# Two attention problems on one core: the gate exponential behind the first scores, first loads in order of need, all partial output sums ahead of the last two key blocks, the flag behind the last evacuations

## The chip, the cores and the metric

The kernel runs on one core of one Trainium2 chip. Times are device microseconds (us) of one execution. A median is over several executions of the same kernel. A profile is the trace of one such execution; its span is about 2 us shorter than the time measured from outside (906.0 for 907.87 us in the profiled run of after).

Engines: PE = TensorE matmul, PEld = TensorE weight load, DVE = VectorE, ACT = ScalarE, POOL = GpSimd, SP = SyncE (a name with q, such as SPq, is that engine's sequencer, which also issues DMAs). In these traces each engine runs its instructions in the order of the program, and an instruction that waits holds up everything behind it (in before, the kA cast, whose input is ready near 9 us, starts at 13.13, behind the gate exp that waits for beta until 13.02).

## The reference, cut to what matters

Two attention layers over 2048 tokens, width 512, 32 heads of 16. Problem A works in 4 segments of 512 with a causal softmax in each, and adds a read from a memory that earlier segments filled. Problem B is plain attention over all 2048 tokens. The outputs stand side by side.

```python
phi = lambda t: jnp.where(t > 0, t + 1.0, jnp.exp(t))
g = sigmoid(beta)                                # one gate per head
for s in range(4):                               # problem A
    p = softmax(qs @ ks.T * scale + mask)
    a_dot = p @ vs
    pq = phi(qs)
    a_mem = (pq @ M) / (pq @ z + 1e-06)          # memory of earlier segments
    outs.append(g * a_mem + (1.0 - g) * a_dot)
    pk = phi(ks)
    M = M + pk.T @ vs                            # first needed in segment 1
    z = z + pk.sum()
...                                              # then @ wo
b = softmax(q @ k.T * scale) @ v                 # problem B, then @ wo
```

## The kernel before

The exponentials of the scores are most of the work of ScalarE. Scores lie in PSUM in two tiles, one of 1536 columns and one of 1024 (the exps of the traces read 128x1536 and 128x1024; the program counts 3 and 2 banks, so a bank in this text is 512 columns), so that PE fills one while ScalarE empties the other. Some score blocks are exponentiated by VectorE with integer arithmetic instead (tiles `v_ps` and `vx`). The program builder keeps a model of time (`T["pe"]`, `T["act"]`, `T["dve"]`, `T["pool"]`) and, while it emits instructions, picks for each gap in PE's work the "chore" (a projection, an evacuation, a memory update) that fits. The result is a fixed order for each engine; nothing is decided on the chip.

The first loads and the start. `ld(queue, which, lo, hi)` loads columns of wq (0), wk (1) or wv (2):

```python
START = 8.4
ARRIVE = dict(wv=13.0, wk=15.3, wq=16.5, xb=(20.5, 26.0, 31.5, 37.0), wvb=24.0)   # model: when loads are there
...
ld(nc.scalar, 1, 0, P)
ld(nc.scalar, 0, 0, P)
xTA = {0: load_xT(wk, "a", 0, "xTA", 1)}         # 4 DMA transposes on SyncE's queue
nc.scalar.activation(warm[:], ones_b[:], ACT.Exp)
load_beta()                                      # 4 small loads, ScalarE's queue
ld(nc.sync, 2)
ld(nc.sync, 1, P)
ld(nc.sync, 0, P)
...                                              # B's weights, 16 DMA transposes of B's x, wo_a, wo_b: all SyncE
for cc in range(4):
    for i in range(2):
        mm(ps0[i][:], wA[1 - i][:, cc, 0:P], xTA[0][:, cc, :], start=(cc == 0), stop=(cc == 3))
pin(nc.scalar.activation(gcol[:], beta_t[:], ACT.Exp, scale=-1.0))     # gate: waits for beta
pin(nc.scalar.copy(kA[0, 0][:], ps0[0][:]))                            # kA: the first scores wait for it
for e in range(2):
    pin(nc.vector.tensor_scalar(qA[0, 0][:, e, :], ps0[1][:], par[:, e:e + 1], None, ALU.mult))
```

The memory's phi(k), which is not part of the change but matters below. `ex` is ScalarE's exp, `po` and `pk` (the tile named phkT) are VectorE's, and four DMA transposes on SyncE's queue turn phkT into `phk` for PE. There is one buffer of phkT; two row tiles of the same segment follow each other through it:

```python
def phase1(wk, src, dst, then):                  # cut: queueing
    ex = wk.tile([P, W], F32, name="ex", tag="ex")
    pin(nc.scalar.activation(ex[:], src, ACT.Exp))
    ...
    pin(nc.vector.tensor_scalar(po[:], src, 0.0, None, ALU.max))
    pin(nc.vector.scalar_tensor_tensor(dst, ex[:], 1.0, po[:], ALU.min, ALU.add))

def do_phik(wk, k, out, then=None):
    pk = wk.tile([P, W], BF16, name="phkT", tag="phkT")
    def move():
        ph = out["ph"] = wk.tile([P, 4, P], BF16, name="phk", tag="phk", bufs=2)
        for kb in range(4):
            nc.sync.dma_start_transpose(ph[:, kb, :], pk[:, kb * P:(kb + 1) * P])
        if then is not None:
            then()
    phase1(wk, k, pk[:], move)
    yield
...
held["pk"] = T["dve"] + 6.5                      # model: the transposes have read phkT by then
...
chore(d - 14, phik(), 1, slot=False, ok=lambda: held["pk"] < T["pe"] and held["ph"] < 2)
```

The end. The partial output sums `l_ps` take PE's time between the last key blocks, and the flag (were all softmax sums in range?) is computed ahead of the last evacuations. All engines load the flag and branch on it to a slow exact path, which these inputs never take:

```python
partial(3, ...); partial(2, ...)
while len(pvq) > 1:
    assert pv(1, True)                           # a key block of the last sums
partial(0, ...)
assert pv(1, True)                               # the last key block
partial(1, ...)
...
run(sums_ok(wk, 62, 64, okm[:, 2:3], "b"))
...
pin(nc.vector.tensor_scalar(flag[:], fps[0:1, 0:1], P - 0.5, None, ALU.is_lt))
for sb in range(4):                              # last evacuations and stores
    ...
```

## Time and profile before

| | before |
|---|---|
| median of the first three runs | 902.09 us (901.56 to 903.89) |
| profiled span | 900.1 us |
| first score exp starts | 14.41 us |
| last score exp ends | 886.94 us |
| from there to the end | 13.14 us |
| score exps on ScalarE / busy time of them | 749 / 856.8 us |

From the profile page of before, a line of the costliest groups (line, engine, operation, tiles, count | busy us, mean ns | idle us just before, and what ended most of it) and two lines of the span in 40 slices of 22.5 us (tenths of busy time; PEclk in tenths of full speed):

```profile
ACT  3899999999999999999999999999999999999994
PEclk8999999999999999999999999999999999999998
L827 ACT ACTIVATE pT<-s_ps 128x1536 bf16<-128x1536 f32 x749 | 856.8, 1287 | 8.3 <-PE s_ps L109 6.1
```

ScalarE is full in all but the first two slices and the last one. So the time is the start of the first exp, plus the exps, plus ScalarE's stalls between them, plus the tail.

The start, from the timeline of before (start us, us, engine, line, operation; in brackets the idle time before and what ended it):

```profile
9.07 1.41 DVE L1069 TENSOR_SCALAR qA<-q_ps,par 128x512 bf16<-128x512 f32 x2 [6.20 <-PE q_ps L109]
...
13.02 0.21 ACT L1066 ACTIVATE gcol<-beta_t 128x8 f32<-128x8 bf16 x1 [9.66 <-DMA beta_t<-in_A_beta_dram]
13.13 0.57 ACT L1067 CAST kA<-k_ps 128x512 bf16<-128x512 f32 x1
...
13.75 1.03 PE L109 MATMUL s_ps<-qA,kA 32*128 32x512 bf16 x6 [4.72 <-ACT kA L1067]
...
14.41 1.45 ACT L827 ACTIVATE pT<-s_ps 128x1536 bf16<-128x1536 f32 x1 [0.71 <-PE s_ps L109]
```

The cast of kA takes 0.57 us and its input was ready near 9 us, but the gate exp in front of it waits 9.66 us for beta. The first scores wait for kA.

The same wait also slows PE, which has nothing to do from 9.0 to 13.7 us: its granted clock falls to half at about 11.1 us (an estimate from one-microsecond windows: 0.56 from 11 to 12, then 0.50) and stays there until about 18 (0.53 from 17 to 18, then 1.00). The windows of PE in before (window, us, busy us and instructions, granted clock, mean DMA share, GB/s):

```profile
16.00:18.00 2.00, 2.00 (x11) 0.52 1.12 167
18.00:20.00 2.00, 2.00 (x14) 1.00 0.54 103
```

The timeline of SyncE's queue in before (the second figure is the time from the first to the end of the last of xN issues):

```profile
18.86 16.11 SPq L219 DMA_TRANSPOSE xT_b<-in_B_x_dram  x12
...
36.26 5.03 SPq L219 DMA_TRANSPOSE xT_a<-in_A_x_dram  x4
49.95 12.11 SPq L315 DMA_TRANSPOSE phk<-phkT  x5
```

And VectorE's timeline in before at the first phi(k):

```profile
48.83 0.28 DVE L289 TENSOR_SCALAR po<-kA 128x512 bf16<-128x512 bf16 x1
49.23 0.69 DVE L290 SCALAR_TENSOR_TENSOR phkT<-ex,po 128x512 bf16<-128x512 f32 x1
49.84 0.71 DVE L358 STREAM_TRANSPOSE tT<-acc 128x512 f32<-128x512 f32 x1
```

SyncE's queue has been done with its loads since 41.3 us (36.26 + 5.03) when phkT is finished at 49.92 (49.23 + 0.69), so the transposes issue at once, at 49.95. The second phkT is written at 60.2, long after they have read the buffer.

The end, from the chain of waits of before (start us, us, what):

```profile
892.69 0.03 DVE flag L1175
...
892.76 0.70 DVE osb L1179
```

The flag is done at 892.83 (its own duration is 0.14 us), and the two evacuations on VectorE come behind it.

### The profile page before, as it was taken

Reading aid. Unit: us, or ns where it says so; the run is one execution under the profiler, and the core shown is the slowest. Engines: PE = TensorE matmul, PEld = TensorE weight load, DVE = VectorE, ACT = ScalarE, POOL = GpSimd, SP = SyncE. Lnnn points to the kernel's source line nnn. Section 1 sums busy time; section 2 is a strip of 40 time slices with the busy share of each in tenths; the row PEclk is TensorE's granted clock in tenths of the full one; section 3 lists DMA queues with packets and bytes.
Section 4 is the critical chain, followed back from the end, with each engine's and each line's share of the span. In section 5 each row is a group of like instructions: output and inputs, shape, how many; then the busy total and the mean of one; then the engine's idle time right before and its main releaser. Section 6 shows DMA issues by size and latency. Waiting matters only on the chain.

```text
span 900.1 us, 18954 instructions
## 1 busy us (share of the span) xinstructions
PE 866.8 (96%) x7674; PEld 260.2 (29%) x7674; DVE 794.2 (88%) x1359; ACT 868.2 (96%) x779; POOL 152.1 (17%) x327
## 2 busy tenths in 40 slices
PE   6999999999999999999999999999999999999996
PEld 2222222232323223222232223223222222222321
DVE  1777789989898998988989999999999899999995
ACT  3899999999999999999999999999999999999994
POOL 4630120411303003030120304002030300000000
PEclk8999999999999999999999999999999999999998
DMA  7700000010000110000000010000000000000001
GB/s 185 143 13 7 24 4 5 7 25 7 7 1 14 36 30 8 1 1 7 1 7 2 25 30 1 1 1 1 2 2 1 19 30 1 2 1 2 1 2 28
DMA packets 35649, 15.47 MB, mean 17 GB/s; under 512 B 27360, under 2 KB 35552, under 8 KB 35552
## 3 DMA queue, kind: packets, MB, share of 16 engines
q1 hardware_dynamic: 33776, 13.78, 6.5%
q8 instruction: 62, 1.02, 0.5%
q10 hardware_dynamic: 1776, 0.40, 0.2%
q14 instruction: 35, 0.29, 0.1%
HBM read 4.20 MB, written 4.19 MB: 9 GB/s over the span
## 4 chain that ended last, share of the span: by engine, by line
PE 42%; ACT 31%; issue 12%; DVE 5%; POOL 2%; DVEq 0%; ACTq 0%; POOLq 0%
ACT pT L827 30%; PE acc L109 19%; PE s_ps L109 11%; PE v_ps L109 7%; POOL pT L837 2%; DVE vx L899 2%; PE o_ps L109 2%; PE k_ps L109 1%; DVE vx L915 1%; ACT ex L284 1%; PE q_ps L109 1%; PE am_ps L109 0%; DVE tT L358 0%; DVE tN L391 0%; POOL qB L259 0%
## 5 line engine op out<-in xcount | busy, mean ns | idle before, releaser
L827 ACT ACTIVATE pT<-s_ps 128x1536 bf16<-128x1536 f32 x749 | 856.8, 1287 | 8.3 <-PE s_ps L109 6.1
L899 DVE TENSOR_SCALAR vx<-v_ps 128x512 uint16<-128x512 f32 x496 | 324.7, 684 | 30.2 <-PE v_ps L109 23.8
L109 PE MATMUL s_ps<-qB,KB 32*128 32x512 bf16 x1552 | 250.7, 382 | 8.9 <-ACT pT L827 5.5
L915 DVE TENSOR_SCALAR vx<-vx 128x2048 uint16<-128x2048 uint16 x372 | 244.6, 690 | 1.9 <-PE acc L109 0.7
L109 PE MATMUL acc<-vx,VB 128*32 128x512 f16 x1984 | 181.3, 385 | 0.6 <-DVE vx L915 0.3
L109 PE MATMUL v_ps<-qB,KB 32*128 32x512 bf16 x496 | 171.4, 382 | 1.1 <-DVE vx L899 0.5
L837 POOL TENSOR_SCALAR_AFFINE_SELECT pT<-pT 128x256 bf16<-128x256 bf16 (+2 forms) x242 | 104.8, 462 | 306.0 <-ACT pT L827 304.7
L109 PE MATMUL acc<-pT,VB 128*32 128x512 bf16 x1552 | 152.8, 387 | 0.0
L109 PEld LDWEIGHTS <-KB 32*128 32x128 bf16 x2048 | 84.2, 91 | 235.8 <-issue 227.8
L109 PE MATMUL acc<-zeros 128*128 128x512 bf16 x411 | 137.1, 386 | 0.0
L109 PEld LDWEIGHTS <-VB 128*32 128x32 bf16 x3536 | 74.5, 94 | 161.7 <-issue 152.4
L109 PE MATMUL s_ps<-qA,kA 32*128 32x384 bf16 (+3 forms) x512 | 54.1, 303 | 7.7 <-ACT kA L1067 4.7
L109 PEld LDWEIGHTS <-zeros 128*128 128x128 bf16 x433 | 35.1, 98 | 84.9 <-issue 77.0
L259 POOL TENSOR_SCALAR qA<-qc,par 128x512 bf16<-128x512 bf16 x24 | 16.5, 701 | 248.6 <-DVE qc L257 248.6
L358 DVE STREAM_TRANSPOSE tT<-acc 128x512 f32<-128x512 f32 x64 | 45.0, 704 | 10.2 <-PE acc L109 9.9
L109 PE MATMUL acc<-pT,vA 128*32 128x256 bf16 (+3 forms) x512 | 32.5, 305 | 1.2 <-DVE vx L899 0.8
L109 PEld LDWEIGHTS <-kA 32*128 32x128 bf16 x512 | 17.1, 92 | 47.8 <-issue 39.7
L259 POOL TENSOR_SCALAR qB<-qc,par 128x512 bf16<-128x512 bf16 x32 | 23.6, 750 | 8.6 <-DVE qc L257 8.6
L435 DVE CAST osb<-o_ps 128x512 bf16<-128x512 f32 x28 | 19.2, 687 | 6.6 <-PE o_ps L109 6.3
L304 DVE CAST vA<-v_ps 128x512 bf16<-128x512 f32 x16 | 11.0, 689 | 11.7 <-PE v_ps L109 11.7
L257 DVE CAST qc<-q_ps 128x512 bf16<-128x512 f32 x28 | 19.2, 684 | 2.4 <-PE q_ps L109 2.1
L109 PE MATMUL k_ps<-xT_a,w_a 128*128 128x512 bf16 x64 | 19.6, 383 | 0.8 <-DMA xT_a<-in_A_x_dram 0.7
(88 smaller groups left out, 419.1 us busy)
## 6 DMA issues: line engine op xcount, KB each, us to landing
out_dram<-osb SPq DMA_DIRECT2D x31, 128.0 KB, 1.7
w_b<-in_B_wqkv_dram SPq DMA_DIRECT2D x3, 512.0 KB, 5.2
phk<-phkT SPq DMA_TRANSPOSE x48, 2.3
w_a<-in_A_wv_dram SPq DMA_DIRECT2D x1, 512.0 KB, 6.6
wo_a<-in_A_wo_dram SPq DMA_DIRECT2D x1, 512.0 KB, 4.3
wo_b<-in_B_wo_dram SPq DMA_DIRECT2D x1, 512.0 KB, 5.1
w_a<-in_A_wk_dram SPq DMA_DIRECT2D x1, 384.0 KB, 7.9
w_a<-in_A_wq_dram SPq DMA_DIRECT2D x1, 384.0 KB, 8.5
```

The lines of the kernel that those rows point to most:

```text
L109: return pin(nc.tensor.matmul(out, lhsT, rhs, **k))
L257: pin(nc.vector.tensor_copy(qc[:], ps[:]))
L259: pin(nc.gpsimd.tensor_scalar(dst[:, e, :], qc[:], par[:, e:e + 1], 0.0, ALU.mult, ALU.add))
L284: pin(nc.scalar.activation(ex[:], src, ACT.Exp))
L304: pin(nc.vector.tensor_copy(dst, ps[:].rearrange("p (h d) -> p h d", d=DH)))
L358: pin(nc.vector.transpose(st["tT"][:, e].rearrange("p c d -> p (c d)"), acc[:]))
L435: pin(nc.vector.tensor_copy(osb[:], ps[:]))
L827: pin(nc.scalar.activation(pT[:, 0:n, :], pt[:, 0:n, :], ACT.Exp, scale=SCALE))
L837: pin(nc.gpsimd.affine_select(out=blk, in_=blk, compare_op=ALU.is_ge, fill=0.0, base=0, pattern=[[0, len(sls)], [1, P]], channel_multiplie ...
L899: pin(nc.vector.tensor_scalar(x[:, j, :], vt[:], XSCALE, float(LADDER[0]), ALU.mult, ALU.add))
L915: pin(nc.vector.tensor_scalar(p[:], x[:], float(off - LADDER[0]), 32767.0, ALU.add, ALU.min))
```

## The change

The intent is to let the first scores start without beta, to bring the first weights in the order in which they are used, to keep VectorE from taking score blocks while it is behind, and to shorten the end. Below, the parts are called the gate (the gate exp behind the sixth score group), the loads (their order, with beta behind them on SyncE's queue), the debt rule (fewer score blocks for VectorE while it is behind), the aT hold (a new aT only when the one buffer is free), the GpSimd rule, the tail order (all partial sums ahead of the last two key blocks) and the flag. The diff, cut to its core:

```diff
+VLATE = 0.5
+TAILPV = 2
-ARRIVE = dict(wv=13.0, wk=15.3, wq=16.5, xb=(20.5, 26.0, 31.5, 37.0), wvb=24.0)
+ARRIVE = dict(w1=11.0, wv=13.5, wk=16.0, wq=17.0, xb=(20.5, 26.0, 31.5, 37.0), wvb=24.0)
@@ loads
-            nc.scalar.dma_start(out=beta_t[...])
+            nc.sync.dma_start(out=beta_t[...])
+        ld(nc.sync, 1, P, 2 * P)
+        ld(nc.sync, 0, P, 2 * P)
+        ld(nc.sync, 2)
+        ld(nc.sync, 1, 2 * P)
+        ld(nc.sync, 0, 2 * P)
         load_beta()
-        ld(nc.sync, 2)
-        ld(nc.sync, 1, P)
-        ld(nc.sync, 0, P)
@@ projections of A, segment 0: row tile 1 may run from w1 on
-    chore(d - LEAD, part(k()), 4, after=rel if s else ARRIVE["wk"], ...)
+    chore(d - LEAD, part(k()), 4, after=rel if s else ARRIVE["w1" if rt == 1 else "wk"], ...)
     ... (the same for q)
@@ score blocks for VectorE: fewer candidates the further it is behind
+    vmin = VMIN + VLATE * (max(0.0, T["dve"] - T["pe"]) + sum(t["us"] for t in tasks)) / QUAD
-    if u["name"] == "a" or len(u["kbs"]) < VMIN:
+    if u["name"] == "a" or len(u["kbs"]) < vmin:
@@ ... (a hold on the one aT buffer; final multiplies may go to GpSimd where the model finds it free)
@@ start
-        pin(nc.scalar.activation(gcol[:], beta_t[:], ACT.Exp, scale=-1.0))
         pin(nc.scalar.copy(kA[0, 0][:], ps0[0][:]))
@@ score loop
-                if t == 3:
-                    later(1.2, gates, prio=1)
+                if t == 6:
+                    pin(nc.scalar.activation(gcol[:], beta_t[:], ACT.Exp, scale=-1.0))
+                    later(1.2, gates, prio=1, ready=on_act(0.2, T["pe"]))
@@ end: partial sums 3 and 2, key blocks down to TAILPV, partial sums 0 and 1, the rest
-        while len(pvq) > 1:
+        while len(pvq) > TAILPV:
             assert pv(1, True)
@@ ...
-        run(sums_ok(wk, 62, 64, okm[:, 2:3], "b"))
-        ... flag
         for sb in range(4):
             ... last evacuations and stores
+        run(sums_ok(wk, 62, 64, okm[:, 2:3], "b"))
+        ... flag
```

Of the GpSimd rule only one multiply comes out in the built program.

More of the change, by code (lines that the diff above doesn't have):

```diff
@@ L58 @@
 POOLMIN = 99
+TAILPV = 2
+POOLTT = 1.2
+POOLSLACK = -99.0
+POOLWITH = 1.2
+POOLWAIT = 4.0
 LEAD = 2.5
@@ L95 @@
     ports = {k: deque(maxlen=8) for k in ("dve", "pool")}
-    held = {"tT": False, "ex": False, "qc": 0, "phi": deque()}
+    held = {"tT": False, "aT": False, "ex": False, "qc": 0, "phi": deque()}
     def mm(out, lhsT, rhs, at=0.0, **k):
@@ L181, in load_beta @@
         for j in range(4):
-            nc.scalar.dma_start(out=beta_t[32 * j:32 * j + 32, :].rearrange("p (rt e) -> p rt e", e=2),
+            nc.sync.dma_start(out=beta_t[32 * j:32 * j + 32, :].rearrange("p (rt e) -> p rt e", e=2),
                               in_=bsrc[j:j + 1].to_broadcast([32, 4, 2]))
@@ L368, in f @@
             if "aT" not in st:
+                held["aT"] = live[0]
                 st["aT"] = wk.tile([P, 2, 16, 32], F32, name="aT", tag="aT")
@@ L372, in f @@
                 then()
-        later(0.72, f, am)
+        later(0.72, f, am, ok=lambda: "aT" in st if e else not held["aT"])
     def fin_pair(wk, st, name, rt, ridx, ot):
@@ L389, in fin_pair @@
         if aT is None:
-            yield -0.75
-            pin(nc.vector.tensor_tensor(o, tT[:, :, :, 0:DH], rr.to_broadcast(bc), op=ALU.mult))
+            eng = (yield (POOLTT, 0.75)) or nc.vector
+            pin(eng.tensor_tensor(o, tT[:, :, :, 0:DH], rr.to_broadcast(bc), op=ALU.mult))
         else:
@@ L397, in fin_pair @@
             t1, t2 = tT[:, :, :, 0:DH], aT[:, :, :, 0:DH]
-            yield -0.7
-            pin(nc.vector.tensor_tensor(t1, t1, rr.to_broadcast(bc), op=ALU.mult))
-            yield -0.7
-            pin(nc.vector.tensor_tensor(t2, t2, r2[:].to_broadcast(bc), op=ALU.mult))
-            yield -0.7
-            pin(nc.vector.tensor_tensor(o, t1, t2, op=ALU.add))
+            eng = (yield (POOLTT, 0.7)) or nc.vector
+            pin(eng.tensor_tensor(t1, t1, rr.to_broadcast(bc), op=ALU.mult))
+            eng = (yield (POOLTT, 0.7)) or nc.vector
+            pin(eng.tensor_tensor(t2, t2, r2[:].to_broadcast(bc), op=ALU.mult))
+            eng = (yield (POOLTT, 0.7)) or nc.vector
+            pin(eng.tensor_tensor(o, t1, t2, op=ALU.add))
         yield 0.71
@@ L555, in project @@
                 if (s, rt) != (0, 0):
-                    chore(d - LEAD, part(k()), 4, after=rel if s else ARRIVE["wk"],
+                    chore(d - LEAD, part(k()), 4, after=rel if s else ARRIVE["w1" if rt == 1 else "wk"],
                           key=("k", "a", s, rt), ok=lambda: s == 0 or ("phk", s - 1, rt) in seen)
-                    chore(d - LEAD, part(q()), 4, after=rel if s else ARRIVE["wq"],
+                    chore(d - LEAD, part(q()), 4, after=rel if s else ARRIVE["w1" if rt == 1 else "wq"],
                           key=("q", "a", s, rt))
@@ L679, in backlog @@
             return max(0.0, T["dve"] - T["pe"]) + sum(t["us"] for t in runnable() if t["ready"] < T["pe"] + 0.6)
+        ptasks = deque()
         def in_turn(g, prio, end=None):
+            on = [None]
             def step():
-                c = next(g, None)
+                eng = on[0]
+                try:
+                    c = g.send(eng)
+                except StopIteration:
+                    c = None
+                ready = max(T["dve"], T["pool"] + 0.06) if eng else T["dve"]
+                on[0] = None
+                if isinstance(c, tuple):
+                    if T["pool"] < T["pe"] + POOLSLACK and len(ptasks) < 2:
+                        on[0] = nc.gpsimd
+                        ptasks.append((ready, c[0], step))
+                        return
+                    c = -c[1]
                 if c is not None:
-                    later(abs(c), step, prio=prio, ready=T["dve"], port=c < 0)
+                    later(abs(c), step, prio=prio, ready=ready, port=c < 0)
                 elif end is not None:
@@ L692, in pair_end @@
             held["tT"] = False
+            if u["name"] == "a":
+                held["aT"] = False
             if u["sums"] == 30:
@@ L920, in pool_run @@
         def pool_run():
+            while ptasks and max(T["pool"], ptasks[0][0]) < T["pe"] + 0.15:
+                free = sum(t["us"] for t in runnable() if not t["port"] and t["ready"] < T["pe"] + 0.3)
+                if live[0] and free < POOLWITH and T["pe"] < ptasks[0][0] + POOLWAIT:
+                    return
+                ready, us, f = ptasks.popleft()
+                on_pool(us, ready)
+                f()
             while T["pool"] < T["pe"] + 0.1:
@@ L1133 @@
                 urge()
-        while chores or cur_chore[0] or tasks or len({q["u"]["id"] for q in pvq}) > 1:
+        while chores or cur_chore[0] or tasks or ptasks or len({q["u"]["id"] for q in pvq}) > 1:
             dve_run(T["pe"])
+            pool_run()
             if cur[0] < len(units) - 1 and pv(1, True):
@@ L1154, in partial @@
                    skip_group_check=True)
-        partial(3, mp.tile([P, D], F32, name="l_ps3", tag="misc")[:])
-        partial(2, mp.tile([P, D], F32, name="l_ps2", tag="misc")[:])
-        while len(pvq) > 1:
+        last = [ps_s.tile([P, BANKS[(NT + i) % 2], 512], F32, name="l_ps", tag=f"s{(NT + i) % 2}") for i in range(1)]
+        left = [(3, lambda: mp.tile([P, D], F32, name="l_ps3", tag="misc")[:]),
+                (2, lambda: mp.tile([P, D], F32, name="l_ps2", tag="misc")[:]),
+                (0, lambda: last[0][:, 0, :]), (1, lambda: last[0][:, 1, :])]
+        for n in (1, 1):
+            sb, t = left.pop(0)
+            partial(sb, t())
+        while len(pvq) > TAILPV:
             assert pv(1, True)
-        last = ps_s.tile([P, BANKS[NT % 2], 512], F32, name="l_ps", tag=f"s{NT % 2}")
-        partial(0, last[:, 0, :])
-        assert pv(1, True)
-        partial(1, last[:, 1, :])
+        for sb, t in left:
+            partial(sb, t())
+        while pvq:
+            assert pv(1, True)
         tN = fin[("b", NSEG - 1, NRT - 1)]["tN"]
@@ L1168 @@
                skip_group_check=True)
-        run(sums_ok(wk, 62, 64, okm[:, 2:3], "b"))
-        okb = wk.tile([P, 1], BF16, name="okb")
-        pin(nc.vector.tensor_reduce(okb[:], okm[:], axis=AX.X, op=ALU.min))
-        fps = ps_a.tile([P, W], F32, name="f_ps", tag="misc")
-        mm(fps[0:1, 0:1], ones_b[:], okb[:], start=True, stop=True)
-        flag = const.tile([1, 1], I32, name="flag")
-        pin(nc.vector.tensor_scalar(flag[:], fps[0:1, 0:1], P - 0.5, None, ALU.is_lt))
         for sb in range(4):
@@ L1183 @@
             (nc.scalar if sb == 2 else nc.sync).dma_start(out=out2[r0:r0 + P, D:2 * D], in_=osb[:])
+        run(sums_ok(wk, 62, 64, okm[:, 2:3], "b"))
+        okb = wk.tile([P, 1], BF16, name="okb")
+        pin(nc.vector.tensor_reduce(okb[:], okm[:], axis=AX.X, op=ALU.min))
+        fps = ps_a.tile([P, W], F32, name="f_ps", tag="misc")
+        mm(fps[0:1, 0:1], ones_b[:], okb[:], start=True, stop=True)
+        flag = const.tile([1, 1], I32, name="flag")
+        pin(nc.vector.tensor_scalar(flag[:], fps[0:1, 0:1], P - 0.5, None, ALU.is_lt))
     def exact_problem(name):
```

## The prediction

> **What bounds the kernel now.** ScalarE's exponentials. In the groups of instructions it is busy 868.2 of 900.1 us, 856.8 of them in 749 exps. In the timeline the first exp starts at 14.41, the last ends at 886.94; between 60 and 880 us the windows show ScalarE 99 to 100% busy. So time = start of the first exp + exp work + ScalarE stalls + tail (13.2 us). Both builds have 749 exps and 124 score blocks exponentiated on VectorE (instruction counts), so the work stays; the change can only move the other three.
>
> **Start.** ScalarE's in-order stream has the gate exp, waiting for the beta loads until 13.02, ahead of the kA cast (13.13) that the first scores (13.75) need. k_ps was done at about 8.9, the first half of qA at about 9.8. With the gate exp six exps later, scores can start at 9.8 and the first exp at about 10.4: 4.0 us gained, all critical.
>
> **Front stalls.** Between 14 and 29 us ScalarE loses about 5.4 us: 1.4 before the third exp (six filler matmuls at 0.43 us, granted clock 0.5 from 11.1 to 17.9 us), 1.05 at 25.6 (mask on GpSimd), 1.74 at 28.2 (k and q of the second row tile, late). The change loads their 128-column weights first and projects them behind the first two score groups. I expect 2 to 4 us of stall left: if the PE clock still halves ([...] here 4.9 us of idle did), seven projection matmuls take 3 us ahead of the third score group; and v waits for wv, now behind 256 KB more, to about 13.3 (12.6 before). Gain 2.5. B's loads slip about 1 us; first use at about 26, landing about 24.5: tight, no stall expected.
>
> **Middle.** Block choice by VectorE's debt, the aT hold and GpSimd finish ops (only one multiply moves in the build) reorder instructions. Stalls from 30 to 850 us total roughly 15 us. Gain 0.5, give or take 2.
>
> **Tail.** Last key blocks ahead of partial sums: the same twelve l_ps matmuls (0.215 us each) and accumulations stand behind the last scores, so the last acc still ends about 2.3 us after the last exp; gain 0 to 0.5. The flag is not harmless at the end. Every engine loads it (892.9), branches (893.5 to 894.6), and resumes only at 896.7 to 898.2. [...] So the span ends by the flag, not by the last store. Behind two 0.69-us evacuations the flag comes 1.5 us later; SyncE, which branched at 894.64 behind its stores, loses only about 0.5. Cost 0.5 to 1.3.
>
> **Sum.** 902.1 - 4.0 - 2.5 - 0.5 + 0.7 = 895.8 us, range 892.5 to 898.8. Faster by over 2% (below 884) 2%, within 2% 97%, slower by over 2% 1%.
>
> **What would show it.** First exp near 10.4; no idle of 9.7 us before the gate exp; ScalarE's waits on PE before 30 us halved; last exp ending near 880; flag to end unchanged at about 7.3 us, last exp to end 13.5 to 14.5.
>
> **What would make it wrong.** Scores still starting late (qA's second half, weights landing after 11 us); B's loads stalling ScalarE after 25 us; new stalls in the reordered middle[...].

## More of the kernel before

ScalarE's timeline around the two phi(k) exps:

```profile
47.93 0.67 ACT L284 ACTIVATE ex<-kA 128x512 f32<-128x512 bf16 x1
...
58.55 0.63 ACT L284 ACTIVATE ex<-kA 128x512 f32<-128x512 bf16 x1
```

## The result, and the profile after

| | before | after |
|---|---|---|
| median | 902.34 us (901.56 to 903.89, 4 runs) | 907.74 us (905.48 to 908.84, 4 runs) |
| profiled span | 900.1 us | 906.0 us |
| first score exp starts | 14.41 | 10.82 |
| last score exp ends | 886.94 | 891.62 |
| from there to the end | 13.14 | 14.43 |

The ratio of after to before is 1.0055, with a 95% interval of 1.0031 to 1.0078: within 2%, but slower. Here and below a ratio is the mean time of one kernel's fast runs over the mean time of the other's fast runs of the same rounds, so it is not quite the ratio of the medians.

The profile page of after, the same three lines:

```profile
ACT  5969999999999999999999999999999999999994
PEclk9979999999999999999999999999999999999998
L853 ACT ACTIVATE pT<-s_ps 128x1536 bf16<-128x1536 f32 x749 | 857.6, 1281 | 15.3 <-PE s_ps L115 12.9
```

The work is the same, 749 exps and 857.6 us. What ScalarE idles ahead of exps has grown from 8.3 to 15.3 us, nearly all of it in waits for scores. The slice strings say where to look: the first slice is better (5 for 3, and a clock of 9 for 8), the third is worse (6 for 9, and a clock of 7 for 9). That is 45 to 67 us.

To see where each microsecond went I took ScalarE's instructions in order and summed, for each stretch, the time from one start to the next beyond the median period of its shape (1.331 us for the 3-bank exp, 0.904 for the 2-bank exp, 0.519 for the phi exp). This balance is worked out from the two traces:

| us | before | after | difference |
|---|---|---|---|
| first exp starts | 14.41 | 10.82 | -3.6 |
| stalls up to 45 us | 5.35 | 1.49 | -3.9 |
| gate exp, now between two score exps | 0 | about 0.5 | +0.5 |
| stalls 45 to 100 us | 2.24 | 10.06 | +7.8 |
| stalls 100 to 870 us | 15.30 | 18.46 | +3.2 |
| stalls behind 870 us | 0.07 | 0.85 | +0.8 |
| last exp to the end | 13.14 | 14.43 | +1.3 |
| sum | | | +6.1 (spans: +5.9) |

A nanosecond more or less in a median period moves the long stretch from 100 to 870 us by some tenths: redone run by run, entries of this kind move by up to 0.5 us, so smaller differences mean nothing.

The start did what it should. Timeline of after, against that of before:

```profile
9.36 0.59 ACT L1099 CAST kA<-k_ps 128x512 bf16<-128x512 f32 x1 [6.00 <-PE k_ps L115]
9.58 1.41 DVE L1101 TENSOR_SCALAR qA<-q_ps,par 128x512 bf16<-128x512 f32 x2 [6.71 <-PE q_ps L115]
10.38 0.59 PE L115 MATMUL s_ps<-qA,kA 32*128 32x512 bf16 x6 [0.84 <-DVE qA L1101]
...
10.82 2.37 ACT L853 ACTIVATE pT<-s_ps 128x1536 bf16<-128x1536 f32 x2 [0.87 <-PE s_ps L115]
```

The wait for beta is gone from the front, PE idles 0.84 us instead of 4.72, and between 8 and 20 us its granted clock stays at 1.00.

Now the third slice. ScalarE's timeline of after around the phi(k) exps:

```profile
30.68 0.67 ACT L290 ACTIVATE ex<-kA 128x512 f32<-128x512 bf16 x1
...
43.72 0.78 ACT L290 ACTIVATE ex<-kA 128x512 f32<-128x512 bf16 x1
44.24 5.70 ACT L853 ACTIVATE pT<-s_ps 128x1024 bf16<-128x1024 f32 x5
54.27 1.45 ACT L853 ACTIVATE pT<-s_ps 128x1536 bf16<-128x1536 f32 x1 [4.34 <-PE s_ps L115]
```

The first phi exp has moved from 47.93 to 30.68 us. Counted in score exps, it stands behind 16 instead of 25, and the second behind 27 instead of 34. Later comes a stall of 4.34 us. SyncE's queue in after:

```profile
19.95 17.94 SPq L225 DMA_TRANSPOSE xT_b<-in_B_x_dram  x12
...
39.18 5.04 SPq L225 DMA_TRANSPOSE xT_a<-in_A_x_dram  x4
44.31 12.94 SPq L321 DMA_TRANSPOSE phk<-phkT  x8
```

VectorE's first phkT of after starts at 33.27 us and takes 0.80. Its transposes come behind loads and issue only at 44.31, 10.2 us later; before, they issued at once. The builder's model lets the second phi(k) come 6.5 us behind the first phkT. VectorE's timeline in after then shows what follows:

```profile
44.70 0.49 DVE L295 TENSOR_SCALAR po<-kA 128x512 bf16<-128x512 bf16 x1
50.82 0.69 DVE L296 SCALAR_TENSOR_TENSOR phkT<-ex,po 128x512 bf16<-128x512 f32 x1 [5.62 <-DMA phk<-phkT]
...
51.92 1.28 DVE L310 CAST VB<-v_ps 128x512 bf16<-128x512 f32 x2
```

The second phkT waits 5.62 us for the transposes to have read the only buffer; the last of the four lands at 50.70. Two evacuations of B's v projections stand behind it in VectorE's order. PE in after stands behind those:

```profile
48.47 0.29 PE L115 MATMUL acc<-pT,vA 128*32 128x256 bf16 x4
52.66 0.41 PE L115 MATMUL acc<-pT,vA 128*32 128x256 bf16 x4 [3.89 <-DVE VB L310]
```

So one DMA wait goes from VectorE to PE (3.89 us) to ScalarE (4.34 us). And the PE clock falls. The same two windows, of all engines (window, us, then busy us and instructions of PE, PEld, DVE, ACT, POOL, then PEclk, DMA share, GB/s), first before:

```profile
50.00:54.00 4.00, 4.00 (x38) 1.19 (x35) 2.71 (x5) 4.00 (x4) 2.95 (x8) 1.00 0.12 25
54.00:62.00 8.00, 7.87 (x60) 2.33 (x58) 5.83 (x10) 8.00 (x9) 2.23 (x7) 1.00 0.03 7
```

and after:

```profile
50.00:54.00 4.00, 1.34 (x8) 0.32 (x7) 2.95 (x6) 0.00 (x0) 0.41 (x1) 0.67 0.08 16
54.00:62.00 8.00, 8.00 (x39) 1.79 (x37) 3.79 (x8) 5.02 (x5) 0.00 (x0) 0.52 0.06 11
```

In the second window PE has work all the time, at half clock. It gets 39 matmuls done where before it did 60, and ScalarE is busy 5.02 of 8 us instead of 8.00. With the slow clock behind it, the wait of 5.62 us costs more than its own length: the stretch from 45 to 100 us loses 7.8 against before.

The end of after, from its chain of waits:

```profile
896.47 0.59 ACT osb L1213
...
897.09 1.29 DVE osb L1211 x2
...
899.36 0.14 DVE flag L1222
```

From the last exp to the end of the flag it is 7.88 us (891.62 to 899.50) instead of 5.89. From the flag to the end of the span it is 6.54 us instead of 7.26, so some of it comes back.

### The profile page after: what moved, and what is told of

Its sections match the earlier page's. It is cut to its first block, busy times and chain, and to the rows that moved or that the text cites. A ratio compares the mean times of both kernels' runs of the same rounds, so it can differ in the third digit from the quotient of the medians.

```text
span 906.0 us, 18918 instructions
## 1 busy us (share of the span) xinstructions
PE 869.2 (96%) x7659; PEld 260.0 (29%) x7659; DVE 795.8 (88%) x1358; ACT 869.4 (96%) x779; POOL 154.8 (17%) x328
## 4 chain that ended last, share of the span: by engine, by line
PE 32%; ACT 16%; DVE 10%; issue 6%; POOL 2%; DMA 0%; ACTq 0%; POOLq 0%; DVEq 0%
PE acc L115 16%; ACT pT L853 15%; PE s_ps L115 8%; PE v_ps L115 5%; DVE vx L926 4%; DVE vx L942 3%; PE o_ps L115 2%; POOL pT L863 1%; DVE osb L442 1%; DVE tT L364 1%; PE q_ps L115 0%; PE k_ps L115 0%; PE l_ps L115 0%; DVE tN L410 0%; DVE aT L408 0%
## 5 line engine op out<-in xcount | busy, mean ns | idle before, releaser
L853 ACT ACTIVATE pT<-s_ps 128x1536 bf16<-128x1536 f32 x749 | 857.6, 1281 | 15.3 <-PE s_ps L115 12.9
L115 PE MATMUL v_ps<-qB,KB 32*128 32x512 bf16 x496 | 175.5, 382 | 2.0 <-DVE vx L926 0.5
L115 PE MATMUL acc<-zeros 128*128 128x512 bf16 x400 | 134.9, 387 | 0.0
L115 PE MATMUL s_ps<-qA,kA 32*128 32x256 bf16 (+3 forms) x512 | 52.6, 299 | 5.0 <-ACT pT L853 2.8
L364 DVE STREAM_TRANSPOSE tT<-acc 128x512 f32<-128x512 f32 x64 | 44.7, 702 | 11.8 <-PE acc L115 11.4
L263 DVE CAST qc<-q_ps 128x512 bf16<-128x512 f32 x28 | 19.2, 685 | 3.5 <-PE q_ps L115 3.0
L115 PE MATMUL o_ps<-wo_a,OT_a 128*128 128x512 bf16 x64 | 19.6, 383 | 0.8 <-DVE vx L926 0.8
```

Source lines behind the costliest of these rows:

```text
L115: return pin(nc.tensor.matmul(out, lhsT, rhs, **k))
L263: pin(nc.vector.tensor_copy(qc[:], ps[:]))
L364: pin(nc.vector.transpose(st["tT"][:, e].rearrange("p c d -> p (c d)"), acc[:]))
L853: pin(nc.scalar.activation(pT[:, 0:n, :], pt[:, 0:n, :], ACT.Exp, scale=SCALE))
```

## The experiments

Two theories went into the runs, and the texts call them A and B (each text says anew what they expect of its run). A: the new load order lets phi(k) come early, while SyncE's queue is still full, and the single phkT buffer turns that into the wait. B: the loss lies in the rest of the reordered schedule (the debt rule, the hold on aT, the new order of work), and the wait for phkT is only where an engine that is late anyway happens to stand. All outputs of all runs were correct.

The table holds the measured results; the stalls are worked out from the traces as above.

| run | median us | ratio to before (95%) | first exp | stalls to 45 | 45-100 | 100-870 | last exp to end |
|---|---|---|---|---|---|---|---|
| before | 902.34 | 1 | 14.41 | 5.35 | 2.24 | 15.3 | 13.14 |
| after | 907.74 | 1.0055 (1.0031-1.0078) | 10.82 | 1.49 | 10.06 | 18.46 | 14.43 |
| e1_own_buffers | 899.92 | 0.9983 (0.9969-0.9998) | 9.88 | 3.25 | 2.31 | 19.35 | 14.69 |
| e2_flag_early | 905.81 | 1.0050 (1.0038-1.0063) | 10.22 | 2.09 | 8.45 | 18.49 | 13.21 |
| e3_gate_only | 896.59 | 0.9947 (0.9932-0.9961) | 10.14 | 4.31 | 2.53 | 15.02 | 13.07 |
| e4_loads_only | 912.44 | 1.0125 (1.0111-1.0140) | 18.99 | 4.15 | 2.34 | 18.98 | 13.88 |
| e5_gate_and_loads | 909.96 | 1.0079 (1.0057-1.0101) | 10.96 | 1.49 | 9.88 | 19.15 | 13.90 |
| e6_gate_loads_buffers | 902.09 | 1.0003 (0.9988-1.0018) | 10.57 | 1.78 | 2.62 | 19.28 | 13.95 |
| e7_buffers_flag_early | 898.87 | 0.9966 (0.9953-0.9980) | 9.57 | 2.26 | 2.71 | 19.48 | 13.01 |
| e8_old_loads | 901.02 | 0.9989 (0.9975-1.0003) | 10.59 | 3.54 | 2.55 | 18.87 | 12.80 |
| e9_hold_phik | 906.97 | 1.0049 (1.0035-1.0064) | 10.44 | 1.94 | 2.54 | 22.99 | 14.73 |
| e10_gate_flag_late | 898.38 | 0.9962 (0.9947-0.9977) | 10.28 | 4.09 | 2.55 | 14.99 | 14.21 |
| e11_gate_again | 897.01 | 0.9946 (0.9931-0.9961) | 10.11 | 4.23 | 2.55 | 15.0 | 13.19 |

The runs came in four jobs (e1 to e4, e5 to e7, e8 and e9, e10 and e11), each with its own runs of before on the same chip, whose medians were 901.17, 901.66, 902.06 and 901.56. The ratios use those.

### e1_own_buffers: the change, with a buffer of its own for each phkT of segment 0

A second buffer from the pool itself does not build (the pool then needs 140.8 KB per partition and 140.1 are left), so segment 0 borrows two buffers that are free then. No instruction moves in the program.

```diff
-    def do_phik(wk, k, out, then=None):
-        pk = wk.tile([P, W], BF16, name="phkT", tag="phkT")
+    def do_phik(wk, k, out, then=None, tag="phkT"):
+        pk = wk.tile([P, W], BF16, name="phkT", tag=tag)
 ...
-    yield from do_phik(wk, kA[s, rt][:], o, moved)
+    yield from do_phik(wk, kA[s, rt][:], o, moved, f"phq{rt}" if s == 0 else "phkT")
```

> The changed kernel, with its instruction order untouched, but the transposed keys phkT of the first segment get a buffer of their own for each row tile (space that lies unused until the second segment), so that VectorE need not wait for the transposing DMAs of the row tile before. Theory A (VectorE stands 5.6 us behind the one phkT buffer, whose DMAs are queued behind the loads, and PE and ScalarE follow): the wait of VectorE on the phk DMA at 45 to 51 us is gone, ScalarE's stalls between 50 and 70 us fall from about 9 to about 1.5 us, time about 900 us. Rival B (B's inputs land too late, or PE lost its clock there for another reason): stall of 7 us or more stays between 50 and 70 us, time 906 to 909.

Measured: 899.92 us against 907.74. The second phkT is written at 45.56 instead of 50.82, and the stalls from 45 to 100 us are 2.31 instead of 10.06. The windows of e1:

```profile
50.00:54.00 4.00, 3.86 (x34) 1.23 (x32) 3.19 (x6) 4.00 (x5) 0.93 (x2) 1.00 0.12 25
54.00:62.00 8.00, 7.95 (x49) 2.33 (x50) 4.93 (x10) 7.74 (x8) 0.00 (x0) 1.00 0.02 4
```

The order of all instructions is that of after, so the order is not what costs here: the one shared buffer is. The half clock goes with the wait: the granted clock is 1.00 in both windows, where after has 0.67 and 0.52. This shows A's mechanism for the 7.8 us.

### e2_flag_early: the change, with the flag ahead of the last evacuations again

```diff
+        run(sums_ok(...)); ... flag          # moved up, as before
         for sb in range(4):
             ... last evacuations and stores
-        run(sums_ok(...)); ... flag
```

> The changed kernel with only its last part undone: the flag is computed ahead of the last evacuations, as before. Theory A [...]: last exp to end falls from 14.4 to about 13.2 us, time about 1 to 1.3 us less (906.4). Rival B (the stores end the span[...]): last exp to end stays at 14.2 or more, time unchanged.

A says of this run that the flag and the branches behind it end the span, B that the stores do.

Measured: 905.81 us, and 13.21 us instead of 14.43 from the last exp to the end. After itself did not run on that chip, so only the trace speaks to the size here; e10 and e11 settle it. The wait for phkT is still there, as it should be (5.87 us). But the stalls from 45 to 100 us are 8.45 us instead of 10.06, with the same order and the same wait: here PE ran at half clock from about 50.2 to 57.0 us, in after from about 51.4 to 61.6 (estimates from one-microsecond windows; the mean granted clock of the whole run was 0.993 here and 0.990 in after). So of these two runs with nearly the same wait (5.87 and 5.62 us), the one whose clock stays low longer loses more.

### e3_gate_only: before, with only the gate exp moved

```diff
-        pin(nc.scalar.activation(gcol[:], beta_t[:], ACT.Exp, scale=-1.0))
         pin(nc.scalar.copy(kA[0, 0][:], ps0[0][:]))
 ...
-                if t == 3:
-                    later(1.2, gates, prio=1)
+                if t == 6:
+                    pin(nc.scalar.activation(gcol[:], beta_t[:], ACT.Exp, scale=-1.0))
+                    later(1.2, gates, prio=1, ready=on_act(0.2, T["pe"]))
```

> The kernel before with one part of the change alone: the gate exp six score groups later (beta still loaded on ScalarE's queue, loads in the old order). Theory A (the start is worth its 3.6 us, all on the critical path; the loss comes from the load order moving the phi(k) chores ahead): first exp at about 10.8, order of the chores as before, no wait of VectorE on phk over 1 us, time 898 to 899. Rival B (an earlier start runs into the loads and is given back by 70 us): first exp at 10.8, but ScalarE's stalls before 70 us grow by 3 us or more, time 901 to 903.

Measured: 896.59 us, ratio 0.9947. PE's order is before's (the trace lacks some matmul records of this run, and all that are there stand in before's order). The first exp starts at 10.14, the stalls up to 45 us fall by 1.0, and nothing else moves (middle 15.02, tail 13.07). The phi exps stand behind 25 and 34 score exps, as before, and no phkT waits. This is the fastest version, and it beats both kernels.

### e4_loads_only: before, with only the new load order

```diff
+ARRIVE = dict(w1=11.0, wv=13.5, wk=16.0, wq=17.0, ...)
+        ld(nc.sync, 1, P, 2 * P); ld(nc.sync, 0, P, 2 * P); ld(nc.sync, 2)
+        ld(nc.sync, 1, 2 * P); ld(nc.sync, 0, 2 * P); load_beta()      # beta on SyncE's queue
 ... (the gate exp stays ahead of kA)
```

> The kernel before with the other part of the start alone: first loads in order of need on one queue, beta behind them, with the arrival table of the changed kernel; the gate exp stays in front. Theory A (this part pulls the first two phi(k) chores 9 and 7 exps forward while the DMA queue is still issuing loads): first exp at 14.5 to 16.5, stalls before 30 us about 1.6 instead of 5.4 us, but VectorE waits on the phk DMA for 2 to 5 us near 48 us and ScalarE stalls by 3 to 6 us behind it; time 902 to 906. Rival B (the stall in the changed kernel comes from the early start, not from the load order): no wait of VectorE on phk, time about 899 to 901.

Measured: 912.44 us, which neither theory had expected. Beta is now the tenth to thirteenth issue of SyncE's queue, and the gate exp, still in front, waits for it. ScalarE's timeline of e4:

```profile
17.60 0.21 ACT L1068 ACTIVATE gcol<-beta_t 128x8 f32<-128x8 bf16 x1 [14.27 <-DMA beta_t<-in_A_beta_dram]
...
18.99 1.45 ACT L829 ACTIVATE pT<-s_ps 128x1536 bf16<-128x1536 f32 x1 [0.71 <-PE s_ps L109]
```

The first exp starts at 18.99. Everything behind shifts with it: the phi exps stand behind 16 and 27 score exps as in after, but phkT is written at 43.6 and 55.6 us, when SyncE's queue is done with its loads, so there is no wait (2.34 us of stalls from 45 to 100). Of the 10.7 us by which the span exceeds before's, 4.6 are the later start and 3.7 the stalls from 100 to 870 us; ScalarE also has four banks more to do (see e6). A had expected a wait of 2 to 5 us, B a time of 899 to 901. The miss is useful: the load order alone moves phi(k) in the instruction order, and the loss from 45 to 100 needs the early start as well.

### e5_gate_and_loads: before, with the gate exp moved and the new load order (e3 and e4 together)

> The kernel before with both parts of the start together (gate exp later, loads in order of need on one queue with the new arrival table) and nothing else of the change. Alone, the gate gave 896.6 us with no wait on phk, the loads 912.4 us with none either (there the late first exp, at 19.0, moved the second phkT write behind the DMA queue's backlog). Theory A (the loss is an interaction: loads move the phi(k) chores forward in the program, the early gate moves them forward in time, and together they meet the backlog that ends at about 44 us): VectorE waits 4 to 6 us on the phk DMA at about 45 to 51 us, ScalarE's stalls from 50 to 100 us come to 8 to 10 us as in the changed kernel, time 904 to 909. Rival B (the stall comes from another part of the change: VectorE's debt rule, the aT hold or the pool ops): no such wait, time 896 to 900.

Measured: 909.96 us. The wait is back, without the debt rule, the aT hold, the tail or the flag of the change. From the waits of e5 from 45 to 65 us (engine, line, what it waited for: us in total, times, longest):

```profile
ACT pT L829 <- PE s_ps L109: 7.1, 5, 4.0
DVE phkT L290 <- DMA phk<-phkT: 5.2, 1, 5.2
```

So two parts of the change, each harmless at this spot, make the loss together: the loads bring phi(k) forward by nine exps, and the gate brings everything forward by four to five microseconds (phkT at 44.4 us in e3, 49.2 in before), into the time when the queue is full.

### e6_gate_loads_buffers: e5 with e1's buffers

> The same two parts, with a phkT buffer for each row tile of the first segment. Theory A: the wait is gone, stalls from 50 to 100 us about 2.3 us, time 898 to 901: 2 to 4 us more than with the gate alone, because this program gives ScalarE two exps (5 banks, some 2 us) more and its reordered middle stalls more. Rival B (the load order is worth its 2 to 3 us of front stalls once the wait is gone): time below 896.

Measured: 902.09 us, ratio 1.0003. With the wait gone, the new load order still takes back all that the gate exp gains. Against e3 the front stalls are 2.5 us better, but the stalls from 100 to 870 us are 4.3 worse (19.28 for 15.02), the tail is 0.9 worse, and the built program has 751 exps instead of 749. In banks of 512 columns ScalarE exponentiates 1876 instead of 1872, since VectorE has one block of four fewer (the text says 5 banks; the trace has one more exp of three banks and one of a single bank). At 1.331 us for three banks, four banks are about 1.8 us, an estimate.

### e7_buffers_flag_early: the change with e1's buffers and e2's flag

> The whole change, with the phkT buffers of the first run and the flag ahead of the last evacuations as before. With the buffers alone it took 899.9 us, ratio 0.9983, and 14.7 us from the last exp to the end. Theory A (the late flag costs 1.2 us, the two repairs add up): last exp to end 13.2 us, ratio about 0.997, time about 898.7. Rival B: last exp to end stays above 14 us, ratio 0.998 or more.

Measured: 898.87 us, ratio 0.9966. The two repairs add up and the result beats before. It does not get below e3 (0.9947; the intervals overlap a little). It starts earlier (9.57) and has fewer front stalls (2.26), and still has 19.48 us of stalls in the middle.

### e8_old_loads: the change with before's loads (and the flag early)

```diff
-ARRIVE = dict(w1=11.0, wv=13.5, wk=16.0, wq=17.0, ...)
+ARRIVE = dict(wv=13.0, wk=15.3, wq=16.5, ...)
 ... (loads and beta as in before; the flag as in e2)
```

> The changed kernel with the old load order and arrival table, and the flag ahead of the last evacuations: what stays of the change is the later gate exp, VectorE's debt rule, the aT hold, the pool ops and the tail order. Its phi(k) chores stand at exps 25 and 34 as in the kernel before; 749 exps, 1872 banks. With the gate alone: 896.6 us, stalls from 100 to 870 us 15.0 us; kernels with the new load order have 18.5 to 19.5 there. Theory A (the new load order also spoils the middle): stalls from 100 to 870 us 14.5 to 16 us, no wait on phk, time 896 to 897.5, ratio 0.994 to 0.996. Rival B (the debt rule spoils the middle too): 18 us or more there, time 899 to 901.

Measured: 901.02 us. The phi exps are back behind 25 and 34, and the 45 to 100 us loss is gone, as A has it. But the middle did not come back to 15: it is 18.87, as B has it. So the rules of the change other than the load order cost 3.9 us of stalls there too. Of this, 3.35 us are one cluster at 204 to 211 us, where PE waits 1.3 us for VectorE and then runs at half clock. PE's windows of e8:

```profile
203.00:205.00 2.00, 1.04 (x12) 0.88 0.00 0
205.00:207.00 2.00, 2.00 (x23) 0.50 0.00 0
```

### e9_hold_phik: the change, with phi(k) kept back to 45 us of the model's time

```diff
-        held.update(pk=0, ph=0)
+        held.update(pk=45.0, ph=0)
```

> The whole change with one number more: the scheduler may not start a phi(k) chore before its own clock says 45 us, when the queue's loads are all issued; one phkT buffer as before. The chores then stand at exps 33 and 42 (16 and 27 in the changed kernel); the program has 751 exps and 1876 banks, 4 more, which cost ScalarE about 1.8 us. Theory A (the buffer's wait needs the chore to be early): no wait of VectorE on phk, stalls from 45 to 100 us 2 to 4 us instead of 10, time 900 to 903. Rival B (something else at 45 to 65 us holds the engines): stalls there of 8 us or more, time above 906.

Measured: 906.97 us where 900 to 903 was expected. The phi exps go behind 33 and 42 score exps, and the wait is gone (2.54 us of stalls from 45 to 100). But the chores behind moved, and a new stall came: fifteen projection matmuls in a row ahead of scores. PE's timeline of e9:

```profile
106.69 3.70 PE L115 MATMUL k_ps<-xT_b,w_b 128*128 128x512 bf16 x15
```

ScalarE loses 3.3 us at 112 behind them, and another 2.7 us at 117.8, where PE does further sums and projections ahead of the scores. The middle has 22.99 us of stalls, and the program one VectorE block of four fewer (1876 banks on ScalarE). The mechanism held; the time did not follow it.

### e10_gate_flag_late and e11_gate_again: e3 with the flag behind the last evacuations, and e3 once more

> The gate-only kernel with the flag moved behind the last evacuations, everything else in the same order: the last part of the change alone, on a program whose runs scatter by only 0.8 us. Theory A [...]: last exp to end 14.4 us instead of 13.1, time 1.0 to 1.5 us above the gate-only kernel of this same job. Rival B [...]: difference under 0.4 us.

> The gate-only kernel again, as the yardstick of the run beside it and to see whether its gain holds on this chip: ratio to the kernel before 0.993 to 0.996, time 896 to 897.5, first exp near 10.2 us, last exp to end 13.1 us. A ratio above 0.997 would say that the first measurement of it was luck.

A says of e10 that the flag and the branches behind it end the span, B that the pause behind the branches shrinks by as much as the flag is later.

Measured on the same chip: 898.38 against 897.01 us, ratios 0.9962 and 0.9946. The late flag costs 1.4 us in medians and 1.0 us in the traces from the last exp to the end (14.21 for 13.19). Why it costs less than its own delay: the span ends with SyncE's last semaphore waits, and they start when SyncE resumes behind its branch. In e10 the flag is done at 890.03, SyncE branches at 890.89 and resumes at 894.30. In e11 the flag is done at 887.88, but SyncE, busy issuing stores, branches only at 889.70 and resumes at 893.26. The flag is 2.15 us later, SyncE's branch 1.2, its resumption and the end 1.0. e11 also repeats e3: 0.9946 and 0.9947.

## Why the prediction was right or wrong

- **What bounds the kernel.** Right. All times follow from first exp, exp work, stalls and tail, and the exp count of after is 749 as before (751 in e4, e5, e6 and e9, which adds about 1.8 us there).
- **Start ("4.0 us gained").** Right: 3.6 us in after, 4.3 in e3, where only this part is done.
- **Front stalls ("Gain 2.5").** Right in kind, larger in size: 3.9 us. The granted clock did not halve; PE's gap shrank from 4.72 us (4.9 in the text) to 0.84, and the clock was 1.00 from 8 to 20 us.
- **Middle ("Gain 0.5, give or take 2").** This is the step that failed, although "new stalls in the reordered middle" stood on my list of what would make it wrong. It was a loss of 11.8 us: 7.8 from 45 to 100 us, 3.2 from 100 to 870 and 0.8 behind that. I treated the reordering as noise around the old order, and looked for collisions of the new load order only among the loads themselves ("B's loads slip about 1 us"). I did not ask what else uses SyncE's queue. The phk transposes do; phi(k) came 17 us earlier (30.68 for 47.93), its transposes stood 10.2 us in the queue, and the model behind the schedule allows 6.5. e1 shows that the shared buffer carries the whole 7.8 us, and e5 that the gate and the loads together produce it. The instruction order of the built program was at hand and showed phi(k) nine exps earlier; reading it against the queue's timeline would have told.
- **The other 3 to 4 us of the middle.** Shown: the new load order alone is enough for it (e5 and e6: 19.2 and 19.3 against 15.0 in e3), the other rules alone are enough too (e8: 18.9), and together they are no worse (after: 18.5). It goes with the instruction order, not with the time of the start: e4, e5 and e6 have the same order behind the start and lose 18.98, 19.15 and 19.28 us there, though their first exps start at 18.99, 10.96 and 10.57. Not shown: why these orders are worse. In e8 most of it is one cluster, while the load-order programs lose it in many places. A guess that no run tests is that any reshuffle of before's order would lose about as much. Nor was it separated which of the debt rule, the aT hold, the GpSimd rule and the tail order makes e8's share.
- **Tail order ("gain 0 to 0.5").** The size is right, though the text has the order the wrong way round: from the last exp's end to the first last evacuation it is 4.85 instead of 4.91 us.
- **Flag ("Cost 0.5 to 1.3").** Right: +1.3 in the traces of after against before, 1.0 to 1.4 in e10 against e11. "Flag to end unchanged at about 7.3 us" was wrong in detail: 6.54. SyncE's stores are already issued when its branch comes, and it resumes 4.6 us after the flag instead of 5.3.
- **Sum.** Without the middle, my terms make -5.8 us (-4.0 - 2.5 + 0.7) and the measured ones -5.7 (-3.6 - 3.9 + 1.3 + 0.5 for the gate exp between score exps, which I left out). The error of 11.9 us (907.74 for 895.8) is the middle, whose term went from -0.5 to +11.8; "last exp ending near 880" showed it at once, with 891.62.

## What to carry to other kernels

When instructions move earlier on one engine, look at every queue and buffer that they use at their new time: the wait came from a DMA queue that carries both loads and a small on-chip transpose, with one buffer between (5.62 us of wait in after). The scheduling model's fixed 6.5 us for the transposes did no harm in before, where they issued at once, and failed in after, where they issued only 10.2 us after phkT was ready. Try each part of a combined change alone as well: here one line (the gate exp) gives 897.0 us, and the whole change 907.7.

One repair suggests itself and was not tried: to send the phk transposes through ScalarE's queue. No run here shows whether it works or what it gains.

## What the traces show of SyncE's queue, the clock and the branch

- The queue. A DMA transpose holds SyncE's queue for 1.23 us (median of the phk issues in after; a plain load about 0.5 us, 0.47 to 0.59 for those of w_a) and lands 2.4 us after its issue. The transposes from HBM (xT_b) take 1.26 us in the median, about 2.5 times a plain load. Twelve of them held the queue for 16.1 us in before and 17.9 us in after, and the phk transposes of after, ready at 34.07, stood behind the last of these, two plain loads and the four transposes of xT_a.
- The clock. In before it fell to half 2.1 us into the gap of 4.72. In e8 PE was busy for 0.71, 0.64 and 0.04 us of the three microseconds from 201 to 204, with a longest gap of 1.3 us, and the clock fell at about 204.5. In after it fell at about 51.4, some 2.6 us into a gap of 3.89, and came back only at about 61.6, 9 us after work had resumed, with PE counted busy all the time. (The moments are worked out from the mean clock of one-microsecond windows, as estimates.) The half-clock stretches were about 3.4 us in e8, 6.8 in before and e2, and 10.2 in after and e5, close to one, two and three times the 3.4 of e8. What sets the moment of the fall and the length of the stretch is not shown.
- The branch. In e10 ScalarE resumed 3.75 us after the flag was done, load and branch included, and in before SyncE resumed 3.5 us after its own branch (894.64 to 898.17). In after SyncE branched at 900.36 and resumed at 904.11; of the DMA traffic from 900.4 to 903.5 us the trace has only five packets, all of the kind "instruction". What the engines wait for in this pause is not shown. The pause, and SyncE's semaphore waits behind it (898.17 to 900.04 in before), set the end of the kernel.
